# Key and state decays on ScalarE, and transposes in other stages, in a fused attention and MLP kernel

## The chip, the cores and the metric

The kernel runs on one core of a Trainium2 chip. The metric is the device time of one execution in microseconds (us). A core has TensorE (PE, with its weight loads shown apart as PEld), VectorE (DVE), ScalarE (ACT), GpSimd (POOL) and SyncE (SP); here POOL and SP only issue transfers.

## The reference

Inputs are q, k, v of 4 batches x 8 heads x 768 positions x 64, one decay `lam` per head, and two matrices of 512x2048 and 2048x512, all float32 inside the kernel.

```
for each block of 64 positions:
    intra = ((qb @ kb^T) * Dmask) @ vb            # Dmask[i,j] = lam^(i-j), i >= j
    inter = (qb * lam^(i+1)) @ kv_state
    out   = intra + inter
    kv_state = lam^64 * kv_state + (kb * lam^(63-i))^T @ vb
x = out as 3072 tokens x 512
h = x @ w_in;  g = h - tanh(h);  result = g @ w_out
```

So each block decays k by `lam^(63-i)` and the state by `lam^64`, one factor per head.

## The kernel before

Six groups g of 512 tokens are worked through (128 positions of each of the 4 batches; a pair of batch and group is a chunk). Each has attention and the MLP. Group 0 is done plainly. For groups 1 to 5 the MLP's products are formed by a seven-product scheme (numbered 1 to 7), some of them by the same scheme again. The loop over g interleaves the MLP of group g with the attention of group n_ = g+1, in these stages:

- **units u0 to u3**: `up(g, u, n)`, products of tokens and w_in for a quarter of the hidden width, 1.73 us of PE each, in banks y and z of PSUM; ACT takes tanh (L558), DVE the sums (L559 to L590). In a unit the order is 6, 5, 1 (of the next unit), 7, 3. Bank z is single: product 5 of a unit can't start before DVE has read product 3 of the unit before (L586).
- **down 1, 2, 4, 5, 6, 7**: products of hidden values and factors of w_out. POOL brings the factors in pieces of 256 KB, seven ahead (L718 to L727).
- **P3**: down product 3 in turn with inner product 2 of the next group (L634).
- **P4**: inner product 4 of the next group, with its first three `up` products between.

The attention of a group goes by pairs of chunks, `first` = (0, 1) and `other` = (2, 3): DVE transposes of q and k (`turned`, L300), q times powers of lam (`faded`, L314), decay of k (`att_decay`, L356, one DVE operation of 128x512 per chunk), `sub_scores` (L403, masked by L407), `sub_state` (L421, then DVE L424 and L425 for the half-way state `mid`), `sub_inter` (L446), `sub_carry` (DVE L480 and L481), `sub_intra` (L463, L472) and, for both pairs, `att_sums`. A table `plan` says after which stage each is written. `spread` is a list of small DVE steps, of which `fill` takes one after each product. The four PSUM banks tagged `att` are shared by scores, state and outputs of the attention.

`load` issues a whole group's loads on SP. For groups 2 to 5, q and k come as block tiles (4 transfers of 112 KB each, L148; 4 buffers, freed by the transposes), and k and v naturally (256 KB, L136; 3 and 4 buffers; a k buffer is freed by `sub_state`). SP keeps the order of the program, but a load may be issued far ahead of its place as soon as its buffer is free. The order of the engines is fixed when the program is built: operations that are `tied` stay behind the one traced before them on their engine, the others go by priority and by when they are thought to be ready.

`sums_once` (L746) forms a difference of hidden values in four DVE operations of 128x512.

Of the kernel before, what the change touches and what calls it, by code (L numbers as in the profile page):

```python
# [16 lines left out]
BLK = 128  # L17
SUBL = 64
GB = 2
# [5 lines left out]
def kernel(  # L25
# [90 lines left out]

    bwd = mask.rearrange("s j p i -> s p j i")[:, :, :, BLK - 1:BLK].to_broadcast([128, NP, 2, D])

    bwd_sub = mask_sub.rearrange("s j p i -> s p j i")[:, :, :, SUBL - 1:SUBL].to_broadcast([128, NP, 2, D])

    lam_blk = fwd[:, :, SUBL - 1:SUBL][:, None, :, :].to_broadcast([128, 2, NP, D])

    def tied(yes, op):
        return tc.keep_in_program_order(op) if yes else op

# [25 lines left out]
    def load(n):  # L151

        while at["loaded"] < min(n, len(chunks)):
            g, b = chunks[at["loaded"]]
            if g < GB:
                raw[g, b] = {}
                load_natural(g, b, "qkv")
                at["loaded"] += 1  # L160
                continue
            for b in range(B):
                raw[g, b] = {}
            for b in range(B):
                load_blocks(g, b, "qk")
                if b == 1:
                    load_natural(g, 0, "kv")
                if b > 0:
                    load_natural(g, b, "kv")
            at["loaded"] += B  # L170


# [152 lines left out]
    def spread(g, bs, what):  # L325

        load(g * B + bs[0] + 1)
        if "t" in what:
            for b in bs:
                for x in "qk":  # L330
                    yield turned(g, b, x)
        if "f" in what:
            for b in bs:
                yield faded(g, b)
        for x, b in zip("01", bs):
            if x in what:
                yield att_decay(g, b)

    def att_scores(g, bs):
        for b in bs:  # L340
# [10 lines left out]
            sc[g, b] = ss  # L351

    def att_decay(g, b):
        kp = raw[g, b]["k"].rearrange("s (p j) d -> s p j d", j=2)
        n, by = (SUBL if g == NG - 1 else BLK), bwd if g == 0 else bwd_sub
        tied(g != 1, nc.vector.tensor_tensor(kp[0:n], kp[0:n], by[0:n], op=AL.mult))  # L356

    def att_state(g, bs):

# [51 lines left out]
    def sub_state(g, bs):  # L411

        subs = range(1 if g == NG - 1 else 2)
        kv = [bank("kv", "att", 4).rearrange("d (b p e) -> d b p e", b=2, p=NP) for _ in subs]
        for n, b in enumerate(bs):
            kd, vn = raw[g, b]["k"], raw[g, b]["v"]
            for p in range(NP):
                for x in subs:
                    for j in range(2):
                        h, r = 2 * p + j, ts(x, SUBL)  # L420
                        nc.tensor.matmul(out=kv[x][ts(j, 64), n, p, :], lhsT=kd[r, h, :], rhs=vn[r, h, :],  # L421
                                         start=n == 0 and p == 0, stop=n == 1 and p == NP - 1, skip_group_check=True)
        st, md = state[:, bs[0]:bs[0] + 2], work.tile([128, 2, NP, D], F32, name="mid", tag="mid", bufs=1)
        nc.vector.tensor_tensor(md, st, lam_blk, op=AL.mult)  # L424
        nc.vector.tensor_tensor(md, md, kv[0], op=AL.add)  # L425
        kvs[g, bs] = kv, md

# [47 lines left out]
    def sub_carry(g, bs):  # L475

        kv, md = kvs.pop((g, bs))
        if g < NG - 1:
            st = state[:, bs[0]:bs[0] + 2]
            nc.vector.tensor_tensor(st, md, lam_blk, op=AL.mult)  # L480
            nc.vector.tensor_tensor(st, st, kv[1], op=AL.add)  # L481

    def att_sums(g, bs):
# [9 lines left out]
    def attention(g):  # L493

        for bs in ((0, 1), (2, 3)):
            att_transpose(g, bs)
            yield
            for b in bs:
                faded(g, b)
                att_decay(g, b)  # L500
            sub_scores(g, bs)
            sub_state(g, bs)
            yield
            sub_inter(g, bs)
            sub_carry(g, bs)
            yield
            sub_intra(g, bs)
        att_sums(g, None)
        yield
# [232 lines left out]

    def sums_once(g, dst, x, y):

        for u in range(NU):
            nc.vector.tensor_tensor(hidden(g, dst)[:, u], hidden(g, x)[:, u], hidden(g, y)[:, u], op=AL.subtract)  # L746

    def down(g, n):

# [211 lines left out]
    for g in range(1, NG):  # L961
        last, n_ = g == NG - 1, g + 1
        if g == 1:
            plan = {"u2": [(sub_scores, n_, first)], "u3": [(sub_state, n_, first)],
                    2: [(sub_inter, n_, first), (sub_carry, n_, first)],
                    4: [(sub_intra, n_, first), (sub_scores, n_, other), (sub_state, n_, other)],
                    5: [(sub_inter, n_, other), (sub_carry, n_, other)],
                    6: [(sub_intra, n_, other), (att_sums, n_, None)]}
        elif not last:
            plan = {"u0": [(sub_state, n_, first), (sub_scores, n_, other)],  # L970
                    "u1": [(sub_inter, n_, first), (sub_carry, n_, first)],
                    "u2": [(sub_intra, n_, first), (sub_state, n_, other)],
                    "u3": [(sub_inter, n_, other), (sub_carry, n_, other)],
                    2: [(sub_intra, n_, other)], 4: [(att_sums, n_, None)]}
        else:
            plan = {}

        def at_place(x):
            fill(16)
            run(plan.get(x, ()))  # L980

        for u in range(NU):
            if g == 1 and u == 2:
                queue.append(spread(n_, first, "tf01"))
            for n in (2, 6, 5, 7, 1, 4, 3) if g < GI else (1, 7, 3) if u == 0 else (6, 5, 1, 7, 3) if u + 1 < NU else (
                    6, 5, 7, 1, 3):
                if n != 1:
                    up(g, u, n)
                elif u + 1 < NU:
                    up(g, u + 1, 1)  # L990
                else:
                    for _ in down(g, 1):
                        fill(1)
                fill(2 if g == 1 and u > 1 else 1)
                if g in turns:
                    made.append(n)
                    step = len(made) - turns[g][0]
                    for t, start in turns[g][1]:
                        if step == start:
                            if t > 1:  # L1000
                                load_quarters(t)
                            making[t] = factors_twice(t)
                        if start <= step < start + 4:
                            next(making[t])
            if g == GI - 1:
                inner_weights(u)
            at_place(f"u{u}")
            if (g, u) == (1, NU - 1):
                queue.append(spread(n_, other, "t0"))
            if not last and g > 1 and u == 1:  # L1010
                queue.append(spread(n_, other, "f1"))
        if twice(g, 4):
            sums_twice(g, 4)
        for _ in down(g, 2):
            fill(1)
        at_place(2)
        if g == 1:
            queue.append(spread(n_, other, "f1"))
        sums_twice(g, 5)
        for _ in down_twice(g, 4, "z") if twice(g, 4) else down(g, 4):  # L1020
            fill(1)
        at_place(4)
        sums_once(g, 21, 21, 11)
        sums_twice(g, 6)
        every(down_twice(g, 5, "w"))
        at_place(5)
        if twice(g, 7):
            sums_twice(g, 7)
        every(down_twice(g, 6, "z"))
        if twice(g, 3):  # L1030
            sums_twice(g, 3)
        at_place(6)
        every(down_twice(g, 7, "w") if twice(g, 7) else down(g, 7))
        if last:
            down_end(g)
            continue
        inner_tokens(n_)
        after = g + 2 if g + 2 < NG else None
        if after:
            queue.append(spread(after, first, "tf01"))  # L1040
        p3 = down_twice(g, 3, "z") if twice(g, 3) else down(g, 3)
        p2 = inner_steps(n_, 2, "yb")
        for kind, _ in in_turn(g):
            next(p3 if kind == "down" else p2)
            fill(1)
        every(p2)
        every(p3)
        fill(16)
        if after:
            sub_scores(after, first)  # L1050
            queue.append(spread(after, other, "t0"))
        p4 = inner_steps(n_, 4, "yb")
        for n in (None, None, 1, None, None, 6, None, None, 5, None):
            if n is None:
                next(p4)
            else:
                up(n_, 0, n)
            fill(1)
        every(p4)
# [30 lines left out]
```

## Time and profile before

| | us |
|---|---|
| runs shown | 679.99, 684.36, 684.20; median 684.2 |
| profiled execution | 681.62, of which the span is 679.8 |
| PE idle within the span | 25.0 (span less busy) |

| engine | busy us | share |
|---|---|---|
| PE | 654.8 | 96% |
| DVE | 495.1 | 73% |
| ACT | 195.7 | 29% |

A row of a group reads: line, engine, operation, output and inputs, shapes, count, then busy time and the mean of one in ns, then idle time of the engine just before and what ended it. A row of the timeline begins with start and length in us. A row of the waits names who waited for whom, then us in total, times, and the longest.

### The profile page before, as it was taken

The numbers are of one execution on the slowest core, as the hardware profiler recorded it, in microseconds if no ns is written. First come the engines' busy times: TensorE is split into PE (matmuls) and PEld (weight loads), VectorE is DVE, ScalarE is ACT, GpSimd is POOL, SyncE is SP. The second block draws the span as 40 slices with busy tenths as digits, with TensorE's granted clock in tenths as the row PEclk, the third lists the DMA queues.
The fourth block names the chain that finished last, engine by engine and source line by source line (L and its number), as shares of the span: only waits on it lengthen the run. The fifth ranks groups of instructions, "written<-read, shape, count | busy, mean of one in ns | idle before, by whom it ended". The sixth has DMA issues, their size and how long they took to land.

```text
span 679.8 us, 15030 instructions
## 1 busy us (share of the span) xinstructions
PE 654.8 (96%) x6104; PEld 566.5 (83%) x6104; DVE 495.1 (73%) x876; ACT 195.7 (29%) x383; POOL 200.0 (29%) x345
## 2 busy tenths in 40 slices
PE   8899999999989799997999999999899999999997
PEld 7688755558878699986899888899888899988897
DVE  4797768994887657598779578788677686357753
ACT  4565334323321111232122234111233311334110
POOL 0001424335422244133266200156300155400351
PEclk9999999999999899998999999999999999999999
DMA  9979979699686978789479954279940268610494
GB/s 212 218 204 250 276 216 310 188 280 281 213 196 172 238 222 227 177 223 272 168 257 275 311 111 97 80 250 273 281 108 1 64 205 287 225 45 1 120 296 157
DMA packets 109541, 135.73 MB, mean 200 GB/s; under 512 B 64289, under 2 KB 81825, under 8 KB 109473
## 3 DMA queue, kind: packets, MB, share of 16 engines
q0 software_dynamic: 28976, 96.49, 46.0%
q1 hardware_dynamic: 80352, 38.29, 25.3%
q8 instruction: 48, 0.79, 0.5%
q14 instruction: 21, 0.16, 0.1%
q10 hardware_dynamic: 144, 0.00, 0.0%
HBM read 110.37 MB, written 24.38 MB: 198 GB/s over the span
## 4 chain that ended last, share of the span: by engine, by line
PE 71%; DMA 11%; DVE 8%; issue 4%; POOL 3%; SPq 2%; ACT 1%; POOLq 0%; DVEq 0%; ACTq 0%
PE y L550 12%; PE z L550 8%; PE y L812 8%; PE h L867 7%; PE zw L812 5%; PE w L759 5%; PE op L888 5%; PE y L759 5%; PE y L634 4%; PE plain L759 3%; DMA wb<-fine_in 2%; PE z L634 2%; DMA fine<-wt 2%; DMA wb<-fine 2%; DMA wb<-factors 2%
## 5 line engine op out<-in xcount | busy, mean ns | idle before, releaser
L724 POOL DMA_DIRECT2D wb<-fine x147 | 79.4, 540 | 97.3 <-PE y L812 34.4
L727 POOL DMA_DIRECT2D wb<-factors x56 | 30.3, 542 | 173.4 <-PE y L759 107.2
L558 ACT ACTIVATE th<-g 128x512 f32<-128x512 f32 x76 | 47.7, 630 | 104.2 <-DVE g L563 43.2
L550 PE MATMUL y<-xt,w 128*128 128x256 f32 x320 | 73.5, 380 | 0.0
L550 PEld LDWEIGHTS y<-xt,w 128*128 128x128 f32 x320 | 59.9, 190 | 9.0 <-ACT g L638 0.9
L559 DVE TENSOR_TENSOR g<-g,th 128x512 f32<-128x512 f32 x76 | 52.0, 687 | 16.7 <-ACT th L558 16.0
L815 ACT ACTIVATE q<-y 128x128 f32<-128x128 f32 x84 | 23.3, 277 | 126.2 <-PE y L812 121.0
L867 PE MATMUL h<-xt,w 128*128 128x256 f32 x256 | 56.5, 381 | 2.1 <-DVE w L268 2.1
L888 PE MATMUL op<-wt,g 128*128 128x512 f32 x128 | 56.8, 596 | 0.0
L867 PEld LDWEIGHTS h<-xt,w 128*128 128x128 f32 x256 | 48.2, 190 | 9.3 <-DVE w L268 1.6
L812 PE MATMUL y<-wb,g 128*128 128x128 f32 x384 | 50.2, 277 | 1.5 <-DMA wb<-fine 1.5
L812 PEld LDWEIGHTS y<-wb,g 128*128 128x128 f32 x384 | 46.2, 192 | 2.3 <-issue 2.0
L888 PEld LDWEIGHTS op<-wt,g 128*128 128x128 f32 x128 | 23.8, 190 | 27.2 <-issue 26.8
L550 PE MATMUL y<-tt,ws 128*128 128x256 f32 x160 | 39.7, 392 | 0.0
L550 PE MATMUL z<-xt,ws 128*128 128x256 f32 x160 | 37.9, 380 | 1.6 <-DVE g L581 1.6
L550 PE MATMUL z<-tt,ws 128*128 128x256 f32 x160 | 38.7, 385 | 0.0
L759 PE MATMUL w<-wb,g 128*128 128x256 f32 x160 | 35.8, 382 | 0.0
L550 PEld LDWEIGHTS z<-xt,ws 128*128 128x128 f32 x160 | 30.3, 190 | 6.1 <-DVE g L581 2.0
L759 PE MATMUL y<-wb,g 128*128 128x256 f32 x160 | 35.3, 379 | 0.0
L195 POOL DMA_DIRECT2D raw<-in_moe_w_out_dram x16 | 8.9, 555 | 87.3 <-DVE g L875 52.4
L550 PEld LDWEIGHTS z<-tt,ws 128*128 128x128 f32 x160 | 30.7, 195 | 4.5 <-DVE g L586 0.2
L759 PEld LDWEIGHTS y<-wb,g 128*128 128x128 f32 x160 | 30.4, 190 | 4.1
(185 smaller groups left out, 1307.2 us busy)
## 6 DMA issues: line engine op xcount, KB each, us to landing
wb<-fine POOLq DMA_DIRECT2D x147, 256.0 KB, 4.0
wb<-factors POOLq DMA_DIRECT2D x68, 256.0 KB, 5.3
raw<-in_moe_w_out_dram POOLq DMA_DIRECT2D x16, 512.0 KB, 5.2
q_blk<-in_q_dram SPq DMA_DIRECT2D x64, 112.0 KB, 6.4
k_blk<-in_k_dram SPq DMA_DIRECT2D x64, 112.0 KB, 6.8
v_nat<-in_v_dram SPq DMA_DIRECT2D x24, 256.0 KB, 6.6
factors<-wt POOLq DMA_DIRECT2D x8, 768.0 KB, 5.7
wb<-fine_in POOLq DMA_DIRECT2D x24, 256.0 KB, 6.0
```

Source lines behind the costliest of these rows:

```text
L195: eng.dma_start(out=dst, in_=moe_w_out[ts(m * KH + n, 128), :].rearrange("k (a n) -> k a n", a=2))
L550: nc.tensor.matmul(out=t[:, m, :], lhsT=wt[:, kt, ts(m, 128)], rhs=x[:, kt, :], start=first and m == 0 and kt == 0, stop=kt == 1, skip_gro ...
L558: nc.scalar.activation(th, src, AF.Tanh)
L559: nc.vector.tensor_tensor(dst(c), src, th, op=AL.subtract)
L634: nc.tensor.matmul(out=dst[:, ts(u, 128)], lhsT=a, rhs=b, start=x in (1, 2, 5) and u == 0, stop=True, skip_group_check=True)
L724: nc.gpsimd.dma_start(out=t.rearrange("p m c -> p (m c)"), in_=fine[TWICE.index(n_), SUB.index(x_)].rearrange("p u c -> p (u c)"))
L727: nc.gpsimd.dma_start(out=t, in_=factors[XAT[FACT[n_][1]]][:, 2 * x_:2 * x_ + 2, :])
L759: nc.tensor.matmul(out=t[:, m, :], lhsT=a[:, u, kt, ts(m, 128)], rhs=wb[:, kt, :], start=first and u == 0 and m == 0 and kt == 0, stop=u = ...
L812: nc.tensor.matmul(out=dst, lhsT=a[:, u, :], rhs=wb[:, ts(u, 128)], start=x in (1, 2) and u == 0, stop=u == NU - 1, skip_group_check=True)
L815: nc.scalar.activation(keep, dst, AF.Copy)
L867: tied(u == 0, nc.tensor.matmul(out=hm[c][:, m, :], lhsT=w1[u][:, i, a, ts(m, 128)], rhs=xt[0, t][:, i, :], start=m == 0 and i == 0, stop= ...
L888: nc.tensor.matmul(out=obank[b], lhsT=g, rhs=wt[:, 2 * a:2 * a + 2, :], start=kt == 0 and a == 0, stop=kt == KH - 1 and a == 1)
```

## The change

The decay of k for groups 1 to 5 becomes eight ACT operations per chunk, one per head, each with a per-partition scale (`decay_head`). The decays of the state (`faded_state`) become four ACT operations, one per pair of heads. Their places are written out (`fade`): chunks 0 and 1 of the group after next in down 6 and 7, chunk 2 in unit 1, chunk 3 in unit 3 (for group 2: unit 2 of loop 1, and after down 2). From loop 1 on, the transposes and fades of q of a group's first pair stand in P4 instead of P3, and in loops 2 to 4 those of the other pair in unit 1 instead of P4 and unit 0; `plan` moves the attention of these loops back by about one stage. Loads of a group go by pairs of chunks (q and k blocks of both, then k and v of both; in group 2 k and v of the first pair come first). `sums_once` uses two operations of 128x1024.

```diff
-    bwd_sub = ...
-    lam_blk = ...
...
-            for b in range(B):
-                load_blocks(g, b, "qk")
-                if b == 1:
-                    load_natural(g, 0, "kv")
-                if b > 0:
-                    load_natural(g, b, "kv")
+            for bs in ((0, 1), (2, 3)):
+                if g == GB and bs[0] == 0:
+                    for b in bs:
+                        load_natural(g, b, "kv")
+                for b in bs:
+                    load_blocks(g, b, "qk")
+                if g != GB or bs[0] > 0:
+                    for b in bs:
+                        load_natural(g, b, "kv")
...
+    def decay_head(g, b, h):
+        n, kp = SUBL if g == NG - 1 else BLK, raw[g, b]["k"]
+        nc.scalar.activation(kp[0:n, h, :], kp[0:n, h, :], AF.Copy,
+                             scale=mask_sub[0:n, h % 2, h // 2, SUBL - 1:SUBL])
+    def faded_state(dst, src):
+        for p in range(NP):
+            nc.scalar.activation(dst[:, :, p, :], src[:, :, p, :], AF.Copy, scale=fwd[:, p, SUBL - 1:SUBL])
...
-        nc.vector.tensor_tensor(md, st, lam_blk, op=AL.mult)
+        faded_state(md, st)
...
-            nc.vector.tensor_tensor(st, md, lam_blk, op=AL.mult)
+            faded_state(st, md)
...
-        for u in range(NU):
-            nc.vector.tensor_tensor(hidden(g, dst)[:, u], ...)
+        for u in range(0, NU, 2):
+            nc.vector.tensor_tensor(hidden(g, dst)[:, u:u + 2], ...)
...
-            plan = {"u0": [(sub_state, n_, first), (sub_scores, n_, other)],
-                    "u1": [(sub_inter, n_, first), (sub_carry, n_, first)],
-                    "u2": [(sub_intra, n_, first), (sub_state, n_, other)],
-                    "u3": [(sub_inter, n_, other), (sub_carry, n_, other)],
-                    2: [(sub_intra, n_, other)], 4: [(att_sums, n_, None)]}
+            plan = {"u0": [(sub_scores, n_, first)], "u1": [(sub_state, n_, first)],
+                    "u2": [(sub_inter, n_, first), (sub_carry, n_, first), (sub_scores, n_, other)],
+                    "u3": [(sub_intra, n_, first), (sub_state, n_, other)],
+                    2: [(sub_inter, n_, other), (sub_carry, n_, other)],
+                    4: [(sub_intra, n_, other)], 5: [(att_sums, n_, None)]}
...
+        def fade(b, g_=n_):
+            load(g_ * B + b + 1)
+            for h in range(0, H, 2):
+                decay_head(g_, b, h)
+                yield decay_head(g_, b, h + 1)
...
+                if g == 1:
+                    fading = {2: (0, 1)}.get(u, ())
+                else:
+                    fading = {1: (2,), 3: (3,)}.get(u, ())
...
-                queue.append(spread(n_, other, "t0"))
-            if not last and g > 1 and u == 1:
-                queue.append(spread(n_, other, "f1"))
+                queue.append(spread(n_, other, "t"))
+            if not last and g > 1 and u == 0:
+                queue.append(spread(n_, other, "tf"))
...
         if g == 1:
-            queue.append(spread(n_, other, "f1"))
+            for b in other:
+                every(fade(b))
+            queue.append(spread(n_, other, "f"))
...
-        if after:
-            queue.append(spread(after, first, "tf01"))
...
         if after:
-            sub_scores(after, first)
-            queue.append(spread(after, other, "t0"))
+            queue.append(spread(after, first, "tf"))
```

Between the last two pieces of the diff stands P3; P4 follows them.

More of the change, by code (lines that the diff above doesn't have):

```diff
@@ L117 @@
     bwd = mask.rearrange("s j p i -> s p j i")[:, :, :, BLK - 1:BLK].to_broadcast([128, NP, 2, D])
-    bwd_sub = mask_sub.rearrange("s j p i -> s p j i")[:, :, :, SUBL - 1:SUBL].to_broadcast([128, NP, 2, D])
-    lam_blk = fwd[:, :, SUBL - 1:SUBL][:, None, :, :].to_broadcast([128, 2, NP, D])
     def tied(yes, op):
@@ L334, in spread @@
                 yield faded(g, b)
-        for x, b in zip("01", bs):
-            if x in what:
-                yield att_decay(g, b)
     def att_scores(g, bs):
@@ L353, in att_decay, with decays @@
     def att_decay(g, b):
-        kp = raw[g, b]["k"].rearrange("s (p j) d -> s p j d", j=2)
-        n, by = (SUBL if g == NG - 1 else BLK), bwd if g == 0 else bwd_sub
-        tied(g != 1, nc.vector.tensor_tensor(kp[0:n], kp[0:n], by[0:n], op=AL.mult))
+        kp = raw[g, b]["k"]
+        tied(True, nc.vector.tensor_tensor(*(kp.rearrange("s (p j) d -> s p j d", j=2),) * 2, bwd, op=AL.mult))
+    def decay_head(g, b, h):
+        n, kp = SUBL if g == NG - 1 else BLK, raw[g, b]["k"]
+        nc.scalar.activation(kp[0:n, h, :], kp[0:n, h, :], AF.Copy,
+                             scale=mask_sub[0:n, h % 2, h // 2, SUBL - 1:SUBL])
+    def decays(g, b):
+        for h in range(H):
+            yield decay_head(g, b, h)
+    def faded_state(dst, src):
+        for p in range(NP):
+            nc.scalar.activation(dst[:, :, p, :], src[:, :, p, :], AF.Copy, scale=fwd[:, p, SUBL - 1:SUBL])
     def att_state(g, bs):
@@ L499, in attention @@
                 faded(g, b)
-                att_decay(g, b)
+                for _ in decays(g, b):
+                    pass
             sub_scores(g, bs)
@@ L743, in sums_once @@
     def sums_once(g, dst, x, y):
-        for u in range(NU):
-            nc.vector.tensor_tensor(hidden(g, dst)[:, u], hidden(g, x)[:, u], hidden(g, y)[:, u], op=AL.subtract)
+        for u in range(0, NU, 2):
+            nc.vector.tensor_tensor(hidden(g, dst)[:, u:u + 2], hidden(g, x)[:, u:u + 2], hidden(g, y)[:, u:u + 2],
+                                    op=AL.subtract)
     def down(g, n):
@@ L980, in at_place @@
             run(plan.get(x, ()))
+        def fade(b, g_=n_):
[3 more added lines that the diff above has]
+                yield decay_head(g_, b, h + 1)
         for u in range(NU):
             if g == 1 and u == 2:
-                queue.append(spread(n_, first, "tf01"))
+                queue.append(spread(n_, first, "tf"))
+            fading = ()
+            if not last:
+                if g == 1:
+                    fading = {2: (0, 1)}.get(u, ())
+                else:
+                    fading = {1: (2,), 3: (3,)}.get(u, ())
+            fading = [x for b in fading for x in [fade(b)]]
             for n in (2, 6, 5, 7, 1, 4, 3) if g < GI else (1, 7, 3) if u == 0 else (6, 5, 1, 7, 3) if u + 1 < NU else (
                     6, 5, 7, 1, 3):
+                for x in fading:
+                    next(x, None)
                 if n != 1:
@@ L1004 @@
                             next(making[t])
+            for x in fading:
+                every(x)
             if g == GI - 1:
@@ L1026 @@
         at_place(5)
+        after = g + 2 if g + 2 < NG else None
+        fading = [fade(b, after) for b in first] if after else []
         if twice(g, 7):
             sums_twice(g, 7)
-        every(down_twice(g, 6, "z"))
+        for _ in down_twice(g, 6, "z"):
+            for x in fading[0:1]:
+                next(x, None)
         if twice(g, 3):
@@ L1032 @@
         at_place(6)
-        every(down_twice(g, 7, "w") if twice(g, 7) else down(g, 7))
+        for _ in down_twice(g, 7, "w") if twice(g, 7) else down(g, 7):
+            for x in fading:
+                next(x, None)
+        for x in fading:
+            every(x)
         if last:
@@ L1037 @@
         inner_tokens(n_)
-        after = g + 2 if g + 2 < NG else None
-        if after:
-            queue.append(spread(after, first, "tf01"))
         p3 = down_twice(g, 3, "z") if twice(g, 3) else down(g, 3)
@@ L1044 @@
             next(p3 if kind == "down" else p2)
-            fill(1)
         every(p2)
         every(p3)
-        fill(16)
         if after:
-            sub_scores(after, first)
-            queue.append(spread(after, other, "t0"))
+            queue.append(spread(after, first, "tf"))
         p4 = inner_steps(n_, 4, "yb")
```

## The prediction

> **What bounds the kernel now.** I read the busy shares, then PE's waits, then stretches of 10 us, then the timeline at each place where PE stood.
>
> ```profile
> PE 654.8 (96%) x6104; PEld 566.5 (83%) x6104; DVE 495.1 (73%) x876; ACT 195.7 (29%) x383; POOL 200.0 (29%) x345
> ```
>
> PE is the bound: 25.0 of 679.8 us are idle, so no edit here can win more than that and the slow matmuls after an idle stretch, since no matmul is removed. DVE at 73% costs only where PE waits for it. PE's waits (us in total, times, longest):
>
> ```profile
> PE kv L421 <- issue: 5.0, 1, 5.0
> PE kv L421 <- DVE k_nat L356: 3.5, 1, 3.5
> PE z L634 <- DMA wb<-fine_in: 3.2, 2, 2.0
> ...
> PE z L550 <- DVE g L581: 1.6, 1, 1.6
> ```
>
> The stretches (start:end; busy us with counts of PE, PEld, DVE, ACT, POOL; granted clock; DMA share; GB/s) show when, and what DMA did then:
>
> ```profile
> 230.00:240.00 10.00, 6.11 (x34) 5.99 (x34) 3.03 (x7) 0.56 (x2) 1.25 (x3) 0.66 0.96 209
> ...
> 310.00:320.00 10.00, 6.52 (x113) 5.26 (x113) 7.75 (x13) 3.31 (x7) 4.29 (x8) 0.88 0.95 267
> ...
> 370.00:380.00 10.00, 8.46 (x74) 8.14 (x74) 7.12 (x12) 1.64 (x4) 4.77 (x10) 1.00 1.05 307
> ...
> 480.00:490.00 10.00, 7.96 (x120) 7.52 (x119) 5.44 (x9) 2.24 (x5) 2.88 (x5) 1.00 1.10 303
> ```
>
> Four places, and three causes. At 370 and 480 (P3 of loops 2 and 3) DMA is full. At 310 (unit 2 of loop 2) DVE is late. At 230 (down 4 of loop 1) PE waited for nothing that the profile shows. After the two longest stands, the clock falls to 0.66 and 0.88; after those of 1.2 and 2.0 us it stays 1.00.
>
> **1. Transposes out of P3.** Each transpose frees a block buffer, and SP then issues a block tile of 4 x 112 KB. In P3 of loop 3:
>
> ```profile
> 470.61 2.09 SPq L148 DMA_DIRECT2D q_blk<-in_q_dram  x4
> 472.80 3.60 SPq L148 DMA_DIRECT2D k_blk<-in_k_dram  x4
> ...
> 480.10 5.70 SPq L148 DMA_DIRECT2D q_blk<-in_q_dram  x4
> ...
> 483.30 1.13 PE L634 MATMUL z<-xt,wb 128*128 128x128 f32 x8 [2.04 <-DMA wb<-fine_in]
> ```
>
> PE uses a 256 KB piece about every 0.89 us there, and the loads compete with the pieces. The four waits of this kind start at 374.50, 378.57, 478.34 and 483.30. At the usual pitch of 0.89 us from the group before they would have started 0.55, 1.32, 0.57 and 2.21 us earlier, and the next group follows 0.08 late each: 4.65 + 0.32 = 5.0 us. In loop 4, whose P3 has no block loads, PE loses 0.24 us to DMA and nothing to `fine_in`. So I take -5.0, bounds -5.0 and 0. The same loads now start in P4 (from 381) and land while units run, where PE needs few pieces: the DMA share at 410 to 440 is 0.30 to 0.35. Without that cover, the price would come back, up to 5.0.
>
> **2. Decays of k and of the state off DVE.** Of 24 L356 (13.5 + 2.6 us) 20 go, 20 x 0.67 = 13.4 us; L424 and L480 go, 6.8 + 5.5 = 12.3; together 25.7 us of 495. Only one of them ended a wait of PE, at 315.35:
>
> ```profile
> 312.69 0.69 DVE L707 TENSOR_TENSOR wt<-wb,wt 128x512 f32<-128x512 f32 x1 [2.09 <-DMA fine<-wt]
> 313.30 0.68 DVE L563 TENSOR_TENSOR g<-g,y 128x512 f32<-128x512 f32 x1
> 313.90 0.68 DVE L424 TENSOR_TENSOR mid<-state,fwd 128x512 f32<-128x512 f32 x1
> 314.74 0.69 DVE L559 TENSOR_TENSOR g<-g,th 128x512 f32<-128x512 f32 x1 [0.16 <-ACT th L558]
> 315.35 0.68 DVE L356 TENSOR_TENSOR k_nat<-k_nat,mask 128x512 f32<-128x512 f32 x1
> ```
>
> The decay stood behind a factor difference (L707) that waited for a write. PE lost 3.48 us, and the two products behind it had pitches of 2.72 and 2.52 against 1.83 and 1.73: 3.48 + 0.89 + 0.79 = 5.2 us. On ACT, idle 307 to 314, the decay is done in time. What is late next is bank z. In unit 1 of loop 2 the transposes are new: 4 at a pitch of 0.95 = 3.8 us. There L586 ended at 303.4 with DVE full but for 0.76 us; L425 (0.6) moves out. So it ends at 303.4 + 3.8 - 0.6 - 0.8 = 305.8. PE wants the next z (304.44 before) earlier, since a state product (0.98) leaves unit 0 and `sub_inter` (1.56) makes room for a state product after unit 1: 304.44 - 1.56 = 302.9. A wait of 2.9 us, with some 0.9 of slow pitch: 3.8. Net -5.2 + 3.8 = -1.4; bounds -5.2 (DVE keeps up) and +2 (it waits for the write, 2.1, as well).
>
> **3. Transposes in unit 1 of loops 3 and 4.** In loop 3 L586 ended at 411.7, the next z came at 413.65. DVE had gaps of 1.52 and 0.75, of which the second waits for a tanh and may stay. The end moves to 411.7 + 3.8 - 0.6 - 1.52 to 2.27 = 412.6 to 413.4; z is wanted at 413.65 - 1.56 = 412.1. Wait 0.5 to 1.3, taken as 0.9, for two loops +1.8; bounds 0 and +7.6 (no gap filled).
>
> **4. `sub_scores` behind `sub_carry` after unit 2.** Scores of the other pair need two of the four `att` banks; two hold outputs, one the second half of the state until L481. In loop 3 `sub_inter` began at 410.26 and L481 ended at 414.1, 3.8 us later, while `sub_inter` lasts 1.56. A fixed order on PE would lose 2.3 us each time, three times; two products (3.5 us) of unit 3 put ahead would lose nothing. The trace shows kv and scores reordered against each other (505.03), so order gives way: +0.3 each, +1.0; bounds 0 and +6.9.
>
> **5. ACT's new work.** The nearest rows are 277 ns for 128x128 from PSUM and 630 ns against 594 for 128x512 from SBUF and from PSUM. The slope (594 - 277)/384 gives 0.83 ns a column, so 128x64 costs about 0.22 to 0.27 and 128x128 about 0.28 to 0.32. 20 chunks x 8 x 0.25 = 40 us, and 18 x 4 x 0.3 = 22 us: ACT rises from 196 to about 258 us, 38%. Behind two decays (0.5 us) stand tanh and evictions, and behind these DVE and PE; in the down stages an eviction has 0.89 us before its bank is wanted. +0.5; bounds 0 and +5, the latter if a decay waits in ACT's queue for its k: k of chunk 2 now follows four block tiles on SP. Starting at 381 with 2 to 2.5 us a tile it is issued near 391 and lands about 6 later, 397; unit 1 wants it at 400. The Trainium skill, in "ScalarE: Activation LUTs" (Rules for kernel authors), sends multiplications to VectorE and not to ScalarE, which speaks against this part; the rows agree that 8 x 0.25 is dearer than 0.68, but ACT idles 71%. By its figures (What ACT_TABLE_LOAD costs: 186 ns, 0.833 ns a column, 93 ns for a pointer scale) 128x64 would be an estimated 0.33 us and ACT's addition some 80 us, which leaves the sum as it is; no row here has a pointer scale.
>
> **6. The rest: nothing on the path.** The wide sums save 20 starts; from 417 ns at 256 columns to 686 at 512, 1024 cost about 1.22 us, so 26.8 falls to 24.4. They serve later stages that show no wait for L746. Near 190 DVE is full and PE loses 1.6 us, but the two decays of that stretch stood behind the late L581 (at 191.66), so the wait stays. The stand at 229 stays too: PE's order up to there is as before, 320 small matmuls and weight loads follow each other in 2.9 us, and DMA is at its limit. The instruction queue moved 48 packets with 0.79 MB, and 12,208 PE instructions over 48 are 254 a packet, so a code fetch fits; no row proves it. "Runtime: NRT & Kernel Launch" (Instruction fetch mechanics) of the Trainium skill holds that crossing a 256-instruction block is mostly hidden; by that rule this place would cost nothing, the trace has 4.96 us.
>
> **Sum.** -5.0 - 1.4 + 1.8 + 1.0 + 0.5 = -3.1 us on the profiled 681.6 (span 679.8 and 1.8 around it): 678.5. That execution lies 2.6 under the median of 684.2; the four executions average 682.5, which gives 679.4. I forecast 679.5.
>
> **Rivals.**
> Faster: DVE's relief carries further, so that unit 1 costs nothing (terms 2 to 5 become -5.2), and the stand at 229, with its slow pitches (1.87, 1.71, 1.48 against 0.89: 7.4 us in all), meets less DMA: 682.5 - 5.0 - 5.2 to -7.4 more, 665 to 672. For it: DVE sheds 28 us. Against: PE's stream and SP's loads at 229 are unchanged.
> Slower: DVE becomes the bound of unit 1. If no gap takes up the four transposes, each of three loops loses 3.8 plus 1.7 of slow clock (as at 316), 16.5 us, against 10.2 won at P3 and at 312: 682.5 + 6.3 = 689. It turns slower above 3.4 us a loop. For it: DVE is at 9.5 to 9.7 of 10 in units 0 and 1 of loop 2. Against: it is at 7.7 to 8.9 in loop 3 (400 to 430).
> Not as meant: P3's waits come from the pieces alone, seven ahead being too few. Then -5.0 is missing: 684.5. Against: loop 4.
>
> **Numbers.** Forecast 0.38, faster 0.30, slower 0.22, not as meant 0.10. One per cent, about what a measurement tells, is 6.8 us: under 677.4 is faster, over 691.0 slower. The forecast's own spread, bounds at half weight, is 674 to 686. Faster by over 1%: 0.30 + 0.07 of the forecast = 0.37. Slower: 0.16 of the slower rival and 0.02 = 0.18. Within: 0.45. The range 668 to 691 leaves out about half of each rival's far side.
>
> **What would show it.** P3 without waits on `fine_in`, and SP's blocks after 380 in loop 2. No L356 after 26 us, and the wait at 312 replaced by one of z for L586 after unit 1. ACT near 258 us, DVE near 467. PE's wait before `sub_scores` after unit 2 under 1 us. The forecast is wrong if decays hold up ACT for k, or if L586 lags over 3.4 us in every loop.

## The result, and the profile after

| | before | after |
|---|---|---|
| median of 8 runs, us | 681.46 (679.59 to 684.36) | 687.35 (684.33 to 689.06) |
| profiled execution, us | 681.62, span 679.8 | 686.37, span 684.6 |
| mean granted clock of PE | 0.992 | 0.988 |

The ratio is 1.0079, 95% interval 1.0052 to 1.0106: 5.9 us slower by the medians. The forecast of 679.5 lay 2.0 us under the median of before; the time is inside its range, on the other side. First the busy shares of after, which answer to the first line shown of before:

```profile
PE 659.9 (96%) x6104; PEld 570.7 (83%) x6104; DVE 470.7 (69%) x818; ACT 254.6 (37%) x615; POOL 199.7 (29%) x345
```

DVE shed 24 us and ACT took on 59, close to what I had worked out (467 and 258). PE is busy for 5.1 us more with the same 6104 matmuls, so some of them ran slower; its idle time is 24.7 us, as before. PE's waits in after:

```profile
PE kv L431 <- issue: 4.8, 1, 4.8
PE sp L413 <- DVE state L491: 4.0, 2, 2.6
PE z L561 <- DVE g L597: 3.0, 1, 3.0
...
PE z L561 <- DVE g L592: 1.6, 1, 1.6
...
PE y L824 <- ACT q L827: 1.0, 1, 1.0
PE zw L824 <- DMA wb<-fine: 0.6, 2, 0.4
```

Gone are the wait of `kv` for the decay of k and the wait for `fine_in`. New are three: the scores (`sp`), which wait for the second half of the state (L491), bank z, and an eviction on ACT (L827). The stretches of after (columns as before: busy us of PE, PEld, DVE, ACT, POOL, granted clock, DMA share, GB/s):

```profile
300.00:310.00 10.00, 7.02 (x62) 5.62 (x55) 9.00 (x15) 5.39 (x15) 3.50 (x6) 0.84 0.94 265
320.00:330.00 10.00, 8.57 (x60) 6.94 (x59) 8.01 (x13) 1.82 (x3) 3.81 (x8) 0.83 0.76 254
370.00:380.00 10.00, 10.00 (x92) 10.00 (x92) 4.04 (x9) 3.07 (x8) 6.32 (x11) 1.00 0.89 291
420.00:430.00 10.00, 7.39 (x171) 6.37 (x170) 8.14 (x14) 4.36 (x12) 0.00 (x0) 0.83 0.45 107
480.00:490.00 10.00, 10.00 (x92) 10.00 (x92) 3.86 (x6) 2.62 (x6) 5.95 (x11) 1.00 0.89 291
```

P3 (370, 480) is now full, at a DMA share of 0.89 instead of 1.05 and 1.10. The three stretches with PE at 7.0 to 8.6 hold the new stands, and the clock falls to 0.83 or 0.84 in each. PE's own timeline shows them, with loop 4 as a control, since the last group carries no state on and its scores have no `sub_carry` before them:

```profile
306.78 3.67 PE L561 MATMUL z<-tt,ws 128*128 128x256 f32 x8 [2.98 <-DVE g L597]
310.29 2.32 PE L561 MATMUL y<-xt,w 128*128 128x256 f32 x10
...
314.27 0.69 PE L456 MATMUL op<-qd,state 64*64 64x64 f32 x32
...
322.33 1.15 PE L413 MATMUL sp<-qt,kt 64*64 64x64 f32 x32 [1.43 <-DVE state L491]
...
420.71 0.69 PE L456 MATMUL op<-qd,state 64*64 64x64 f32 x32
...
422.16 1.09 PE L413 MATMUL sp<-qt,kt 64*64 64x64 f32 x30
425.86 1.67 PE L413 MATMUL sp<-qt,kt 64*64 64x64 f32 x34 [2.61 <-DVE state L491]
427.46 3.07 PE L561 MATMUL y<-tt,ws 128*128 128x256 f32 x8
...
432.10 1.24 PE L561 MATMUL y<-xt,w 128*128 128x256 f32 x5
...
528.68 0.69 PE L456 MATMUL op<-qd,state 64*64 64x64 f32 x32
...
530.13 1.11 PE L413 MATMUL sp<-qt,kt 64*64 64x64 f32 x64
...
534.73 1.89 PE L561 MATMUL y<-xt,w 128*128 128x256 f32 x8
```

From the first product of `sub_inter` to the third product behind the scores loop 4 takes 534.73 - 528.68 = 6.05 us, loop 3 takes 432.10 - 420.71 = 11.39: the scores cost loop 3 5.3 us, of which the stand itself is 2.6. In loop 2 the order did give way (two products and the start of a third stand between the two halves of the scores), and 1.43 us of stand were left.

Why L491 came so late in loop 3 is on DVE and ACT. ACT, and then DVE, in after:

```profile
421.89 0.68 ACT L366 ACTIVATE state<-mid,fwd 128x128 f32<-128x128 f32 x2
422.81 0.63 ACT L569 ACTIVATE th<-g 128x512 f32<-128x512 f32 x1 [0.23 <-DVE g L597]
423.34 0.68 ACT L366 ACTIVATE state<-mid,fwd 128x128 f32<-128x128 f32 x2
```

```profile
423.23 1.28 DVE L313 TENSOR_TENSOR qd<-qt,fwd 128x512 f32<-128x512 f32 x2
424.44 0.68 DVE L570 TENSOR_TENSOR g<-g,th 128x512 f32<-128x512 f32 x1
425.04 0.68 DVE L491 TENSOR_TENSOR state<-state,kv 128x512 f32<-128x512 f32 x1
```

The four decays of the state stand on both sides of a tanh, and L491 behind two fades of q. It ended 5.0 us after `sub_inter` began; before the change that was 3.8.

**Where the time went.** I numbered the matmuls of the MLP, which are the same in both kernels, and took how far the nth lies behind that of before, less what either had run by then of the attention's small matmuls and the other had not (0.0165 us each, from 0.53 us per 32).

| stretch of after | lag at its start and end, us | what lies there |
|---|---|---|
| 244 to 250, down 4 to 5 of loop 1 | -0.5 to 0.8 | eviction L827 behind decays on ACT |
| 303 to 311, unit 1 of loop 2 | 0.5 to 5.5 | wait of z, and the slow clock behind it |
| 313 to 320, unit 2 of loop 2 | 5.5 to 0.5 | the wait at 312 of before, and its slow clock, gone |
| 320 to 328, unit 3 of loop 2 | 0.5 to 4.4 | scores |
| 376 to 385, P3 of loop 2 | 4.7 to 2.5 | waits on `fine_in` gone |
| 417 to 434, unit 3 of loop 3 | 2.7 to 7.9 | scores |
| 444 to 473, downs of loop 3 | 7.9 to 8.9 | not traced further |
| 482 to 497, P3 of loop 3 | 8.9 to 5.8 | waits on `fine_in` gone |
| 497 to the end | 5.8 to 4.8 | small differences |

### The profile page after: what moved, and what is told of

Its sections match the earlier page's. It is cut to its first block, busy times and chain, and to the rows that moved or that the text cites. A ratio compares the mean times of both kernels' runs of the same rounds, so it can differ in the third digit from the quotient of the medians.

```text
span 684.6 us, 15206 instructions
## 1 busy us (share of the span) xinstructions
PE 659.9 (96%) x6104; PEld 570.7 (83%) x6104; DVE 470.7 (69%) x818; ACT 254.6 (37%) x615; POOL 199.7 (29%) x345
## 4 chain that ended last, share of the span: by engine, by line
PE 67%; issue 15%; DVE 6%; DMA 4%; POOL 4%; SPq 2%; ACT 1%; POOLq 0%; DVEq 0%; ACTq 0%
PE y L561 10%; PE y L824 8%; PE op L900 8%; PE h L879 7%; PE zw L824 6%; PE z L561 6%; PE y L645 4%; PE y L771 3%; PE w L771 3%; POOL wb L735 3%; PE plain L771 2%; PE z L645 2%; DMA wb<-fine 2%; DMA k_nat<-in_k_dram 1%; DVE g L570 1%
## 5 line engine op out<-in xcount | busy, mean ns | idle before, releaser
L561 PE MATMUL y<-xt,w 128*128 128x256 f32 x320 | 74.9, 384 | 0.0
L827 ACT ACTIVATE q<-y 128x128 f32<-128x128 f32 x84 | 23.2, 277 | 121.7 <-PE y L824 118.2
L356 ACT ACTIVATE k_nat<-k_nat,mask 128x64 f32<-128x64 f32 (+1 forms) x160 | 41.0, 335 | 13.3 <-DMA k_nat<-in_k_dram 13.3
```

Source lines behind the costliest of these rows:

```text
L356: nc.scalar.activation(kp[0:n, h, :], kp[0:n, h, :], AF.Copy, scale=mask_sub[0:n, h % 2, h // 2, SUBL - 1:SUBL])
L561: nc.tensor.matmul(out=t[:, m, :], lhsT=wt[:, kt, ts(m, 128)], rhs=x[:, kt, :], start=first and m == 0 and kt == 0, stop=kt == 1, skip_gro ...
L827: nc.scalar.activation(keep, dst, AF.Copy)
```

## The experiments

Theories at the outset: the place of the scores behind `sub_carry` takes the time (the place theory); ACT's decays, some of which wait for their k, hold up what stands behind them on ACT (the queue theory); the stand at 229 comes from the burst of small matmuls there and not from DMA (the burst theory). The letters in the expectations are those of each text. Times are medians; each ratio is to runs of before on the same chip.

| run | us | ratio |
|---|---|---|
| after | 687.35 | 1.0079 |
| e1 scores later | 683.11 | 1.0024 |
| e2 before with the decays on ACT | 682.47 | 1.0009 |
| e3 after with the decays on DVE | 681.33 | 1.0009 |
| e4 before with loop 1's burst split | 676.53 | 0.9924 |
| e5 = e1 + e3 + e4 | 673.39 | 0.9862 |
| e6, e9 = e1 with ACT's decays in P4, untied and tied | 682.54, 679.75 | 1.0010, 0.9959 |
| e7 = e1 with loop 2's transposes later | 684.39 | 1.0031 |
| e8 before with the new loads and sums | 683.42 | 1.0022 |
| e10, e12 = e5 with P3's transposes back in loop 1, in all | 681.04, 685.14 | 0.9986, 1.0049 |
| e11 = e10 with the decays on ACT | 682.13 | 0.9988 |
| e13 = e9 + e4 | 673.70 | 0.9894 |
| e14 = e1 + e3 | 677.21 | 0.9936 |

### e1, scores later

After, with this plan for loops 2 to 4:

```diff
-                    "u2": [(sub_inter, n_, first), (sub_carry, n_, first), (sub_scores, n_, other)],
-                    "u3": [(sub_intra, n_, first), (sub_state, n_, other)],
-                    2: [(sub_inter, n_, other), (sub_carry, n_, other)],
-                    4: [(sub_intra, n_, other)], 5: [(att_sums, n_, None)]}
+                    "u2": [(sub_inter, n_, first), (sub_carry, n_, first)],
+                    "u3": [(sub_intra, n_, first), (sub_scores, n_, other)],
+                    2: [(sub_state, n_, other)], 4: [(sub_inter, n_, other), (sub_carry, n_, other)],
+                    5: [(sub_intra, n_, other)], 6: [(att_sums, n_, None)]}
```

> The changed kernel, but in loops 2 to 4 the scores of the other pair move from after unit 2 to after unit 3 (behind the outputs of the first pair), and what follows them goes one stage later. Theory A (the bank that sub_carry frees too late): PE's two stands before the scores after unit 2 of loops 2 and 3 vanish with the slow clock behind them, 3.2 + 5.1 = 8.3 us in the profile of the changed kernel; its 687.3 becomes about 679, below before's 681.5. Rival B (DVE is simply behind in units 1 and 2, the scores only showed it): PE stands instead at bank z or at the state products, and the time stays within 3 us of 687.

Measured: 683.11 us, ratio 1.0024 (0.9993 to 1.0054). Both stands before the scores are gone, yet the median is only 4.2 us under that of after, half of what Theory A expected: PE's waits on evictions on ACT (L827) rose from 1.0 to 4.8 us, with a new one of 2.9. ACT in that run, two rows:

```profile
344.81 0.83 ACT L356 ACTIVATE k_nat<-k_nat,mask 128x64 f32<-128x64 f32 x3 [4.25 <-DMA k_nat<-in_k_dram]
345.54 0.25 ACT L827 ACTIVATE q<-y 128x128 f32<-128x128 f32 x1
```

The decay had waited 4.25 us for its k, and the eviction behind it (345.54) ended PE's wait of 2.92 us. So the place theory holds for the two stands, and the queue theory shows itself as soon as the place is mended.

### e2, the decays alone

Before, with the decays of k (groups 1 to 5) and of the state on ACT, and nothing else:

```diff
-        tied(g != 1, nc.vector.tensor_tensor(kp[0:n], kp[0:n], by[0:n], op=AL.mult))
+        for h in range(H):
+            nc.scalar.activation(raw[g, b]["k"][0:n, h, :], raw[g, b]["k"][0:n, h, :], AF.Copy,
+                                 scale=mask_sub[0:n, h % 2, h // 2, SUBL - 1:SUBL])
...
-        nc.vector.tensor_tensor(md, st, lam_blk, op=AL.mult)
+        faded_state(md, st)
```

> The kernel before, with the decays of k (groups 1 to 5) and of the state on ScalarE at the places where VectorE did them; nothing else changed. If the decays are harmless and only their neighbours cost: the stand of 3.5 us at 312 (decay behind a factor difference on VectorE) is gone with its slow clock, 5.2 us: about 676. If ScalarE's new work itself is what costs (evictions and tanh behind 8 operations per chunk, sub_carry in four pieces): no gain, 681 to 686, with PE waiting for ScalarE's copies.

Measured: 682.47 us, ratio 1.0009 (0.9984 to 1.0033). DVE fell to 472.6 us and the stand at 312 went, but PE then waited 3.3 us for copies on ACT (L587). ACT in this run:

```profile
297.11 2.02 ACT L360 ACTIVATE k_nat<-k_nat,mask 128x64 f32<-128x64 f32 x8 [4.35 <-DMA k_nat<-in_k_dram]
299.04 0.57 ACT L587 ACTIVATE g<-y 128x512 f32<-128x512 f32 x1
```

The queue that waits for the k has moved from DVE to ACT, and the wait with it.

### e3, the change with the decays on DVE

```diff
-        nc.scalar.activation(kp[0:n, h, :], kp[0:n, h, :], AF.Copy, scale=mask_sub[...])
+        if h == 0:
+            tied(g != 1, nc.vector.tensor_tensor(kq[0:n], kq[0:n], bwd_sub[0:n], op=AL.mult))
...
-        for p in range(NP):
-            nc.scalar.activation(dst[:, :, p, :], src[:, :, p, :], AF.Copy, scale=...)
+        nc.vector.tensor_tensor(dst, src, lam_blk, op=AL.mult)
```

> The changed kernel, with the decays of k and of the state put back on VectorE as whole operations, at the changed places. If sub_carry is late because ScalarE does it in four pieces among tanhs, the stand before the scores after unit 2 of loop 3 shrinks by 1 us or more and the time falls below 687. If VectorE's load decides, its 26 us come back, the stand at bank z after unit 1 of loop 2 grows beyond 3.0 us, those before the scores stay or grow, and the time is 688 to 695.

Measured: 681.33 us, ratio 1.0009 (0.9981 to 1.0037). PE's waits of this run:

```profile
PE sp L415 <- DVE state L493: 3.4, 2, 2.5
PE y L563 <- DVE g L582: 3.0, 2, 2.5
```

The scores wait here too (0.88 and 2.50 us, where after has 1.43 and 2.61), so it is their place and not the engine of the decays that makes them wait; the time fell as the first theory has it, but the stand of loop 3 shrank by 0.1 us and not by 1. PE and DVE in e3, loop 3:

```profile
417.51 0.69 PE L458 MATMUL op<-qd,state 64*64 64x64 f32 x32
```

```profile
423.23 0.68 DVE L493 TENSOR_TENSOR state<-state,kv 128x512 f32<-128x512 f32 x1
```

The second half of the state (L493 here) ended 6.4 us after `sub_inter` began, later than the 5.0 of after: with no pieces on ACT it stood behind sums and fades on DVE alone. Yet the median of e3 is 6.0 us, and its span 5.4 us, under that of after. The stands of after are longer by 2.5 us (0.6 before the scores, 1.0 on L827, 0.9 at 229), and after has two more stretches of 3.41 us at a granted clock of 0.50, which cost up to half their length, 1.7 us, each. Not all of this is shown to come from ACT: the stand at 229 varies from 3.9 to 5.1 us in the kernels that have it, with either engine.

### e4, the burst of loop 1 split

Before, with the state products of the other pair one stage later in loop 1:

```diff
-                    4: [(sub_intra, n_, first), (sub_scores, n_, other), (sub_state, n_, other)],
-                    5: [(sub_inter, n_, other), (sub_carry, n_, other)],
-                    6: [(sub_intra, n_, other), (att_sums, n_, None)]}
+                    4: [(sub_intra, n_, first), (sub_scores, n_, other)], 5: [(sub_state, n_, other)],
+                    6: [(sub_inter, n_, other), (sub_carry, n_, other), (sub_intra, n_, other),
+                        (att_sums, n_, None)]}
```

> The kernel before, but in loop 1 the run of 160 small products (outputs, scores, state) after down 4 is split: the state of the other pair moves behind down 5, its outputs behind down 6. If the stand of 5.0 us at 229 is PE running out of fetched code in that run, it goes, with the slow clock behind it: 7.4 us less, about 674. If it is something else at that time (a load, a bank), it stays at about 229 or moves, and the time stays at 681.

Measured: 676.53 us, ratio 0.9924 (0.9892 to 0.9957), 5.0 us under before by the medians. The stand is gone, at a DMA share of 1.07 to 1.12 there, higher than before. PE in this run:

```profile
224.82 0.69 PE L463 MATMUL op<-ss,v_nat 64*64 64x64 f32 x32
225.35 1.21 PE L403 MATMUL sp<-qt,kt 64*64 64x64 f32 x64
226.48 1.16 PE L812 MATMUL y<-wb,gS 128*128 128x128 f32 x8
```

Here 96 small matmuls with their weight loads pass without a stand; 160 in a row made one of 3.9 to 5.1 us in each of the ten kernels that have them. (In e5, where 96 and 32 stand with two larger products between them, 0.94 us of such a stand is left at 248.) The burst theory holds. That the missing thing is PE's own instructions fits this (nothing else that PE could wait for is late), but no row proves it.

### e5, the parts together

e3's decays, e1's plan and e4's split in one kernel, with the transposes as in after.

> After, with the decays of k and of the state on VectorE in wide instructions again, with the scores of the other pair after unit 3, and with loop 1's scores and state products of the other pair in separate stages. Theory A (the transposes out of P3 are worth 5.1 us; the rest of what the change lost comes from the place of the scores and from ScalarE's decays): the run with VectorE's decays stood at 681.3; without its stands before the scores (0.9 and 2.5 us, 3.4 us plus at most one slow window of 1.7) it is 676 to 678, and without the stand at 229 (5.0 to 6.8) 670 to 673; ratio 0.982 to 0.988. Rival C (the parts do not add, since each moved stand lets another come or shifts the slow windows): 675 or above, ratio 0.990 or above, with new stands of over 1 us on PE elsewhere.

Measured: 673.39 us (672.69 to 673.77), ratio 0.9862 (0.9829 to 0.9895): faster than both kernels, and the lowest median of the study. No scores wait for a state. What is left of PE's waits:

```profile
PE y L563 <- DVE g L582: 3.0, 2, 2.5
...
PE zw L826 <- DMA wb<-fine: 1.2, 1, 1.2
PE z L563 <- DVE g L599: 1.0, 1, 1.0
```

### e6 and e9, ACT's decays given out later

e6 is e1 with the decays of the first pair written in P4 instead of downs 6 and 7. e9 is e6 with those decays `tied` (t is true for them alone).

```diff
-        fading = [fade(b, after) for b in first] if after else []
+        fading, late_fading = [], [fade(b, after) for b in first] if after else []
...
             fill(1)
+            for x in late_fading:
+                next(x, None)
```

```diff
-        nc.scalar.activation(kp[0:n, h, :], ...)
+        tied(t, nc.scalar.activation(kp[0:n, h, :], ...))
```

> After with the later scores, and with ScalarE's decays of the next group's first pair given out in P4 in place of downs 6 and 7 (their loads are asked for where they were). Theory B (a decay that waits for its k holds the evictions behind it in ScalarE's queue, and that took back what the later scores won): the stands of y on ScalarE's eviction L827 (4.8 us in three, longest 2.9) fall under 1.5 us together; 683.1 falls by 3.3 to 6 (3.3 of stand, up to two slow windows of 1.7), to 677 to 680. Rival (the evictions are late for another reason, such as ScalarE's greater share of busy time): these stands stay over 3 us and the time stays within 1.5 of 683.1.

> The run with ScalarE's decays given out in P4, and now kept in the order written, so that nothing may put them among the evictions of downs 6 and 7 (which it did at 343.25 and 344.13). Theory B (decays that wait for k stand in front of evictions): the three stands of y on L827 (1.0, 1.3, 0.9 us) go, 3.3 us with 0 to 1.7 of slow clock: 682.5 becomes 677.5 to 679.5. Rival: the evictions wait for something else, and stands of 0.9 us or more stay there; time within 1.5 of 682.5.

e6: 682.54 us, ratio 1.0010 (0.9981 to 1.0039), a miss: 3.3 us of stands on L827 were left. ACT in e6 shows why:

```profile
343.25 0.82 ACT L356 ACTIVATE k_nat<-k_nat,mask 128x64 f32<-128x64 f32 x3 [2.59 <-DMA k_nat<-in_k_dram]
343.98 0.25 ACT L827 ACTIVATE q<-y 128x128 f32<-128x128 f32 x1
```

P4 of that loop comes over 30 us later. The decays were written there, but untied operations are ordered by when they are thought to be ready, and they went back among the evictions. e9: 679.75 us, ratio 0.9959 (0.9935 to 0.9983); PE has no wait on L827 at all. The queue theory holds: 2.8 us by the medians (3.5 by the ratios, since the chips differ), for three stands of 3.3 us together.

### e7, loop 2's transposes one unit later

e1 with the other pair's transposes in unit 2 of loop 2 instead of unit 1:

```diff
-            if not last and g > 1 and u == 0:
+            if not last and g > 1 and u == (1 if g == 2 else 0):
```

> After with the later scores, and in loop 2 the transposes of the other pair given out in unit 2 in place of unit 1 (loops 3 and 4 as in after). Theory D (the four transposes in the full VectorE of loop 2's unit 1 make the stand of z behind g L597 of 3.0 us and its slow window): that stand goes, 683.1 falls by 3.0 to 4.8, to 678.3 to 680. Rival (VectorE is as full in unit 2, which holds a factor difference that waits for its write): a stand of 2 to 4 us behind VectorE comes at 308 to 325 in its place, time within 1.5 of 683.1.

Measured: 684.39 us, ratio 1.0031 (1.0001 to 1.0062). The rival holds. PE in this run:

```profile
320.59 3.51 PE L561 MATMUL z<-tt,ws 128*128 128x256 f32 x8 [3.09 <-DVE g L597]
```

The stand moved one unit on, at the same size, and a stand of 1.46 us on an ACT copy came before it.

### e8, loads and wide sums alone

Before, with the loads by pairs and the wide `sums_once`, as in the diff of the change.

> Before with only the loads by pairs of chunks and the wider sums of the change. My forecast for these two was nothing on the path: ratio 0.998 to 1.002. The wider sums take about 2.4 us off VectorE's busy time. If the order of the loads matters (k and v of the first pair come after fewer blocks, those of the second after more), waits of the state products or of decays for k_nat change by over 1 us.

Measured: 683.42 us, ratio 1.0022 (0.9998 to 1.0046). A ratio of 1 lies inside the interval, at its edge. The wide sums took 24.3 us where the narrow ones took 26.8, as I had worked out. The wait on the decay at 312 is 3.2 us, and those on `fine_in` sum to 4.5, where before had 3.5 and 3.2.

### e10 to e12, the transposes put back in part

e10 is e5 with the transposes for loop 2 beside P3 and P4 of loop 1, as before the change. e11 is e10 with the decays on ACT, kept as in e9. e12 is e5 with the transposes put back in all loops (its condition is `after` alone).

```diff
+        early_turn = after and g == 1
+        if early_turn:
+            queue.append(spread(after, first, "tf"))
...
             next(p3 if kind == "down" else p2)
+            if early_turn:
+                fill(1)
...
+        if early_turn:
+            fill(16)
+            queue.append(spread(after, other, "t"))
```

> The combined run, but the transposes for loop 2 are given out as before the change (first pair beside P3 of loop 1, other pair beside its P4); loops 2 and 3 stay as changed. Theory D (what remains is VectorE in unit 1 of loop 2, which holds factor differences and the moved transposes): the stand of y behind g L582 at 299.7 (2.5 us) and the slow window after it (1.7) go, nothing on fine_in comes in P3 of loop 1 (it had none before): 673.4 - 4.2 = 669.2, range 668 to 671. Rival: P3 of loop 1 gets waits on fine_in of 1 to 3 us, or VectorE is late elsewhere before 310: 672 or above.

> As the run before in this list, with the decays of k and of the state on ScalarE, kept in the order written in P4. Theory E (once nothing waits behind them, ScalarE's decays are worth what VectorE's waits are worth, which is by then nothing): within 1.5 us of the run before in this list. Rival F (VectorE is still late in places, so ScalarE's decays win): 1.5 to 4 us under it. Rival G (ScalarE's decays hold others up even so): over it by more than 1.5, with stands of PE on ScalarE.

> The combined run, but with the transposes beside P3 and P4 as before the change in all loops. Theory A (the transposes out of P3 are worth 5.1 us in loops 2 and 3): against the run that keeps them there in loop 1 alone, it is 4 to 7 us slower, and PE's waits on fine_in (3 to 5 us) are back in P3 of loops 2 and 3, at about 370 and 475. Rival (the loads by pairs, or the earlier plan, had already taken that competition away): within 1.5 us, and no waits on fine_in.

e10: 681.04 us, ratio 0.9986 (0.9965 to 1.0007), 12 us above the 669.2 that I expected and 7.7 above e5. The stand of y at 299.7 went, but one of z, 1.97 us, came before 291.79, and one of 5.1 us on a factor piece ended at 320.87, with 6.83 us at half clock from 319.6 on. POOL's order had changed. POOL in e10:

```profile
312.38 1.51 POOL L731 DMA_DIRECT2D wb<-factors  x2
313.89 0.56 POOL L721 DMA_DIRECT2D fine<-wt  x1
314.86 1.14 POOL L740 DMA_DIRECT2D wb<-factors  x2 [0.41 <-DVE wb L720]
```

In e5 two pieces (L740) are issued at 312.29, where here two transfers of `load_quarters` (L731) are. That this alone makes the stand wasn't tried. So e10 could not say what the stand at 299.7 costs.

e12: 685.14 us, ratio 1.0049 (1.0018 to 1.0080). It has the same new stand, so it is compared with e10: 4.1 us slower, within the 4 to 7 expected. PE's waits in e12 have the line back that the change took away:

```profile
PE z L647 <- DMA wb<-fine_in: 3.5, 2, 2.0
```

e11: 682.13 us, ratio 0.9988 (0.9961 to 1.0014); by the ratio no different from e10. Both carry the stand of over 5 us, so two more runs were made without it.

### e13 and e14, the engines of the decays compared again

e13 is e9 with e4's split: all of the change, mended. e14 is e5 without the split.

> The run with ScalarE's decays kept in P4, and loop 1's burst split as in the combined run. Theory (with nothing behind a waiting decay, the engine of the decays is worth less than 1.5 us, and the split is worth the 5 us it won alone): 679.75 - 5.0 = 674.7, range 673 to 676; within 1.5 of the combined run's 673.4; PE has no stand on L827. Rival (ScalarE's decays cost by themselves): 676.5 or above. Rival (they win): 671.9 or below.

> The combined run without the split in loop 1: the change with VectorE's decays and the later scores alone. Theory: 673.4 + 5.0 to 6.8 = 678.4 to 680.2, within 1.5 of 679.75 (the run with ScalarE's decays kept in P4), with the stand at 229 of about 4 to 5 us and no stand before the scores. Rival (the split lets something else come, so that it is worth less here): below 677.

e13: 673.70 us (673.19 to 677.77), ratio 0.9894 (0.9856 to 0.9932), against 0.9862 for e5 on DVE. e14: 677.21 us, ratio 0.9936 (0.9906 to 0.9966), against 0.9959 for e9 on ACT. In neither pair is ACT better, and in each the intervals overlap. The Trainium skill ("ScalarE: Activation LUTs", Rules for kernel authors) gives multiplications to VectorE, and here nothing spoke for the other engine.

Four kernels differ in two things alone, the place of the scores and the engine of the decays: after (neither moved), e1 (scores later), e3 (decays on DVE) and e14 (both). The place is worth 4.2 us with ACT's decays and 4.1 with DVE's, the engine 6.0 in the old place and 5.9 in the new one, by the medians; by the ratios, which allow for the chips, 3.8 and 5.0, and 4.8 and 6.0. So the engine cost the change about as much as the place, or more. Where ACT's decays are pinned as well (e9 against e14), 2.5 us of that are left, 1.6 by the ratios.

## Why the prediction was wrong

**The step that failed is 4, "so order gives way: +0.3 each".** It forecast +1.0, and the lag of after grew by 9.1 us in its places (3.9 in loop 2, 5.2 in loop 3, 0 in loop 4), above its upper bound of 6.9. I had worked out the price of a fixed order, 2.3 us each, and dropped it for one place (505.03) where two matmuls of the scores stand among the last of kv. The stands were 1.4 and 2.6 us; one place where an order gave way by a few matmuls is no proof for another. The step also counted three such places where there are two, since loop 4 has no state to carry. The bound was broken because I had left out what follows a stand: after both, PE ran 3.41 us at a granted clock of 0.50. e1 shows the cause of the stands: with the scores elsewhere, both are gone. It doesn't show that the place alone costs 9.1 us. Moving the scores won 4.2 and moving the decays back to DVE 6.0 (e3), so a second step failed beside it: term 5 had ACT's new work at +0.5.

**Term 1.** Transposes out of P3, forecast -5.0: measured -2.2 and -3.1 in loops 2 and 3, together -5.3, and e12 against e10 gives 4.1. Right, and with the mechanism named: no P3 of after waits on `fine_in`, and in loop 2 SP issues the blocks after 385.

**Term 2.** Decays off DVE, forecast -5.2 + 3.8: measured -5.0 and +4.9. The wait of z for L597 was forecast as 2.9 us and measured as 2.98; its slow clock was 1.8 us instead of 0.9. The gain did not need ACT, though: in e3, e5 and e14 DVE does the decays at the changed places, and PE waits for none of them.

**Term 3.** Transposes in unit 1 of loops 3 and 4, forecast +1.8: measured 0. DVE had room there; with the decays on DVE as well (e14) 0.97 and 0.47 us of waits appear.

**Term 5.** ACT's new work, forecast +0.5, "+5, the latter if a decay waits in ACT's queue for its k": +1.3 in the lag of after, for an eviction at 246.9 behind eight decays of k and two pieces of the state's, none of which waited for a load. By e3 it was 6.0 us, most of it in longer stands and slow stretches elsewhere, as told there. The bad case is real too: ACT waited 13.3 us for k in after, mostly where nothing stood behind. Where something did, it cost PE 2.3 of the 3.3 us in e2 and 3.8 of the 4.8 us in e1.

```profile
L356 ACT ACTIVATE k_nat<-k_nat,mask 128x64 f32<-128x64 f32 (+1 forms) x160 | 41.0, 335 | 13.3 <-DMA k_nat<-in_k_dram 13.3
```

This row of the costliest groups in after also settles the size of a decay: mean 335 ns, while eight in a row take 2.02 us, a pitch of 0.24. The 0.25 from the slope of two rows was right as the price of one in a row.

**Term 6.** The rest at nothing: the waits near 190 and at 229 stayed as forecast, and e8 shows nothing beyond its interval.

By the lag the terms are -5.3 - 0.1 + 0 + 9.1 + 1.3 = +5.0, with -0.2 left for the rest, against +4.8 between the spans. With terms 4 and 5 at nothing the sum would be -5.4, where I had forecast -3.1. e14, the kernel with the later scores and DVE's decays, measured 5.4 us under before (682.57 on the same chip), an agreement that is partly chance, as its waits in loop 2 are others; e9, with ACT's decays pinned, measured 1.6 under.

Of the rivals, the one that ended slower named another cause: DVE as the bound of unit 1 in three loops. It came true in loop 2 alone, where the forecast had it too. "Not as meant" is refuted by P3. The faster rival spoke of the stand at 229 meeting less DMA; e4 shows the stand gone under more DMA, so that reason was wrong as well.

What stays open: the stand of some 3 us that DVE makes in loop 2 (z in after, y in e5). e7 moved it, e10 traded it for another, and no run took it away. Also not traced is 1.0 us in the downs of loop 3.

## What to carry to other kernels

Before work is moved behind another step, look for what the two share besides data: here a PSUM bank that is free only at the end of a chain of operations on other engines; a fixed order is the price to take until the trace shows that same pair giving way. An operation that may wait for a load belongs in a queue, and at a place in it, where nothing urgent stands behind; and if a scheduler orders the queue, pin the place, since writing it later may change nothing (e6 against e9). One of the largest gains, 5.0 us (e4), came from a stand that the change did not touch: 160 small matmuls in a row, split in two.

## What was not expected of the hardware

Short stands cost PE's clock. The stretches of after and of e13 below hold the same wait of z, 2.98 and 3.05 us, and then the 3.4 us behind it (columns as above). After:

```profile
303.80:306.80 3.00, 0.02 (x2) 0.02 (x1) 3.00 (x6) 0.00 (x0) 0.89 (x2) 1.00 1.02 280
306.80:310.20 3.40, 3.40 (x8) 2.77 (x9) 2.40 (x4) 2.54 (x9) 0.70 (x2) 0.50 0.98 289
```

e13:

```profile
300.50:303.60 3.10, 0.05 (x1) 0.00 (x0) 3.10 (x6) 0.00 (x0) 0.91 (x2) 1.00 1.07 284
303.60:307.00 3.40, 3.40 (x16) 3.01 (x17) 0.55 (x1) 1.20 (x4) 0.73 (x2) 1.00 0.91 250
```

After the same stand, PE ran at 0.50 in the one, with 8 matmuls in 3.4 us, and at 1.00 in the other, with 16. In all traces the slow stretches, but for the one in which each run ends, last 3.41 or 6.83 us and lie whole multiples of 3.41 us apart within a run, from a start that differs from run to run; so a stand of 2 to 3 us seems to cost the clock when most of it falls into one such stretch, and not when two share it about evenly (2.50 us in e3 at 421.56 were followed by no slow stretch). The wait of 1.43 us in loop 2 did cost it, with 1.1 us of small 64x64 products behind it. The Trainium skill ("TensorE: Matmul & The Clock Gate", Part 1: The HAM clock gate) describes such a free-running window of 3413 ns, which the rows bear out; its rule, idle gaps of no more than about 3.4 us, was not enough here, where 2.6 us in after was followed by half clock. This is read from the traces of the sixteen kernels; no run set the phase, so it was not isolated by an experiment.
